# Fixed places for each expert's tokens, with stationary weights, in a state-space scan followed by a top-1 mixture of experts

## The chip, the cores and the metric

The kernel runs on one core of a Trainium2 chip. The core has five engines with queues of their own: TensorE (PE for its matmuls, PEld for its weight loads), VectorE (DVE), ScalarE (ACT), GpSimd (POOL) and SyncE (SP). The metric is the device time of one execution in microseconds (us).

## The reference

The first half is a Mamba-2 scan over 4 sequences of 768 steps with 8 heads, head width 32 and state width 16. The second half routes each of the 3072 tokens to one of 8 experts, which is a two-layer network of width 1024.

```python
# scan, by chunks: y = (C B^T * decay) x  +  (C state) * decay ;  state = decay * state + B^T x
x = attn_out.transpose(0, 2, 1, 3).reshape(3072, 256)      # a token's row
logits = x @ w_gate                                          # 256 -> 8
expert_idx = np.argmax(logits, axis=1)
gate_w = softmax(logits)[np.arange(N), expert_idx]
for e in range(8):
    mask = expert_idx == e
    h = np.maximum(x[mask] @ w1[e], 0.0)                     # 256 -> 1024
    out[mask] = gate_w[mask, None] * (h @ w2[e])             # 1024 -> 256
```

The inputs are drawn with a fixed seed. Everything is fp32 except the counts of the routing.

## The kernel before

**The scan.** The 3072 tokens are 24 chunks of 128. A written-out loop issues, for each chunk: decay factors (`decay`: matmul `abc`, then a VectorE scan into `L`), score products (`scores`: `g` from `ctm` and `bt`), `dec` and `ctd` (`decay_in`), `bs` (`scaled_B`), the mask of the next chunk (`masks`: `ctm`), the state (`state`), the output of the chunk before (`y`), the weighting of `L` (`weigh`), and for the chunk before that the rows by token with their logits (`rows`). GpSimd makes `ctm`, `ctd` and `bs`. Loads come in groups of three chunks on SP's queue, two groups ahead, and the 16 weight matrices (1 MB each) go in the same queue behind them.

**The routing.** For each six chunks `choose` finds the expert and the gate, and SP's queue writes the six chunks' rows to `x_hbm` in token order; two chunks later `rank` numbers the tokens within their experts, with eight VectorE instructions that end in `A_all`.

**The seam.** After the last chunk `table` counts tiles of 128 tokens for each expert and builds, with 24 small matmuls, `idx`: the token in each place of up to 31 tiles, and `ei`, the expert of each tile.

**The experts.** 31 tiles are always run. For each, GpSimd gathers 128 rows by `idx` (`m_gather`, L355), TensorE reads the expert's number into a register (`m_e`, L359) and transposes the rows (`m_xT`, L365), the first product keeps the transposed rows stationary and moves 512 columns of weights (`m_h`, L374), TensorE transposes the result (`m_hT`, L382), the second product keeps the transposed result stationary and moves 256 columns of weights (`m_y`, L389), ACT applies the gate (L392) and GpSimd scatters the rows to the output (L393). TensorE's order is: first product of tile j, transposes of tile j + 1, transposes of h of tile j - 1, second product of tile j - 2. Each fp32 matmul of the code stands in the trace as two instructions, a transpose as one.

Of the kernel before, what the change touches and what calls it, by code (L numbers as in the profile page):

```python
# [9 lines left out]
FP32 = mybir.dt.float32  # L10
# [21 lines left out]
def ssd_then_moe(ctx, tc, x, a, B, BT, CT, w_gate, w1, w2, out):  # L32
    nc = tc.nc
    x_hbm = nc.dram_tensor("x_hbm", (N + 1, W), FP32, kind="Internal").ap()
# [14 lines left out]
    w_all = wpool.tile([128, E, 2, KT * F], FP32, name="w_all")  # L49
# [10 lines left out]
    iota_b = consts.tile([128, 128], BF16, name="iota_b")  # L60
    iota_f = consts.tile([128, 32], FP32, name="iota_f")
    rev_e = consts.tile([128, E], FP32, name="rev_e")
    hi_f = consts.tile([128, NT], FP32, name="hi_f")
    lo_f = consts.tile([128, 1], FP32, name="lo_f")
    zrow = consts.tile([1, W], FP32, name="zrow")

    oh_all = route.tile([128, NT, E], BF16, name="oh_all")
    cnt = route.tile([128, NT + 1, E], BF16, name="cnt")
    rhi_all = route.tile([128, NT], FP32, name="rhi_all")
    A_all = route.tile([128, NT, 128], BF16, name="A_all")  # L70
    idx = route.tile([128, NTILE], I32, name="idx")
    ei = route.tile([1, NTILE], I32, name="ei")

# [13 lines left out]
    def route_consts():  # L87
        nc.gpsimd.memset(Tmat, 1.0)
        nc.gpsimd.affine_select(out=Tmat, in_=Tmat, pattern=[[1, 128]], base=-1, channel_multiplier=-1,
                                compare_op=ALU.is_ge, fill=0.0)  # L90
        nc.gpsimd.memset(ones_bf, 1.0)
        iota_i = sm.tile([128, 128], I32, name="iota_i")
        nc.gpsimd.iota(iota_i, pattern=[[1, 128]], base=0, channel_multiplier=0)
        nc.vector.tensor_copy(iota_b, iota_i)
        nc.vector.tensor_copy(iota_f, iota_i[:, 0:32])
        nc.vector.tensor_scalar(out=rev_e, in0=iota_f[:, 0:E], scalar1=-1.0, scalar2=float(E),
                                op0=ALU.mult, op1=ALU.add)
        nc.vector.tensor_scalar_add(hi_f, iota_f[:, 0:NT], 1.0)
        lo_i = sm.tile([128, 1], I32, name="lo_i")
        nc.gpsimd.iota(lo_i, pattern=[[0, 1]], base=0, channel_multiplier=1)  # L100
        nc.vector.tensor_copy(lo_f, lo_i)
        nc.vector.memset(zrow, 0.0)
        nc.vector.memset(cnt[:, 0, :], 0.0)
        nc.sync.dma_start(out=x_hbm[N:N + 1, :], in_=zrow)

# [29 lines left out]
    def load_w(i):  # L135
        e, u = divmod(i, 2)
        nc.sync.dma_start(out=w_all[:, e, u, :], in_=(w1, w2)[u][e])
# [12 lines left out]
    def decay(k):  # L150
# [3 lines left out]
        for t in range(2):  # L154
# [3 lines left out]
            # L[j, h, i]: the product of a over the steps j + 1 .. i, 1 at i = j, 0 before  # L158
# [73 lines left out]
    rt = [dict() for _ in range(NT // RG)]  # L232

    def rows(k):
# [5 lines left out]
        # columns: features 0 .. 127, logits, features 128 .. 255; the logits add up over both halves  # L240
# [10 lines left out]
    def choose(g):  # L251
# [9 lines left out]
        # of equal logits the first expert  # L261
# [13 lines left out]
        n0 = g * RG * 128  # L275
        nc.sync.dma_start(out=x_hbm[n0:n0 + RG * 128, :].rearrange("(c p) w -> p c w", p=128), in_=r["rows"])

    def rank(g):
# [5 lines left out]
        rk = sm.tile(sh, FP32, name="rk")  # L284
        nc.vector.tensor_tensor(out=rk, in0=p, in1=oh_all[:, sl, :], op=ALU.mult)
# [215 lines left out]
```

## Time and profile before

| | us |
|---|---|
| median of 3 timed runs | 429.83 |
| lowest and highest | 429.77, 429.99 |
| span of the profiled execution | 423.2 |
| TensorE busy (matmuls) | 392.9 |
| VectorE busy | 185.5 |
| GpSimd busy | 115.0 |
| ACT busy | 69.7 |

The span runs from the first to the last instruction of the profiled execution. The page gives no other time for that execution; the timed runs lie 6.6 to 6.8 us above its span. Busy time counts the instructions of an engine, not its waits, and TensorE's matmuls overlap, so that their cost is better read from start to start.

### The profile page before, as it was taken

How to read it: one execution, taken by the hardware profiler on the slowest of the kernel's cores; microseconds unless marked ns; L12 is line 12 of the kernel's file. 1: busy time of each engine (PE TensorE's matmuls, PEld its weight loads, DVE VectorE, ACT ScalarE, POOL GpSimd, SP SyncE). 2: the span in 40 equal slices, each digit the busy share in tenths (PEclk: the TensorE clock that was granted, in tenths of full speed). 3: DMA queues.
4: the chain of work that ended last, by engine and by line, in shares of the span. 5: the costliest groups of instructions: out<-in, count | busy, mean ns of one | idle time of the engine just before them, and what ended most of it. 6: DMA issues, size and time to landing. Idle time of an engine off the chain costs nothing.

```text
span 423.2 us, 5415 instructions
## 1 busy us (share of the span) xinstructions
PE 392.9 (93%) x1879; PEld 247.0 (58%) x1879; DVE 185.5 (44%) x328; ACT 69.7 (16%) x163; POOL 115.0 (27%) x172
## 2 busy tenths in 40 slices
PE   5999999999999813999999999999999999999995
PEld 1355455554554402467767767767767767767773
DVE  5699898889888862113113113113112112112220
ACT  1011110211111210112112112112112112112110
POOL 2333341343333114011231131131131132131011
PEclk9999997998988965899999999999999999999999
DMA  6978859759002021001011010011011011111000
GB/s 192 324 273 323 319 151 363 228 220 254 2 0 76 0 75 51 26 12 39 24 39 35 25 39 28 26 37 30 25 33 39 25 37 37 26 25 29 12 2 0
DMA packets 14498, 37.04 MB, mean 88 GB/s; under 512 B 2278, under 2 KB 9641, under 8 KB 12426
## 3 DMA queue, kind: packets, MB, share of 16 engines
q1 hardware_dynamic: 11498, 29.48, 20.6%
q0 software_dynamic: 2976, 7.23, 6.0%
q8 instruction: 16, 0.26, 0.3%
q14 instruction: 8, 0.07, 0.0%
HBM read 30.40 MB, written 7.22 MB: 89 GB/s over the span
## 4 chain that ended last, share of the span: by engine, by line
issue 53%; PE 17%; POOL 13%; DVE 10%; DMA 4%; POOLq 1%; ACT 0%; SPq 0%; DVEq 0%
POOL xs L355 7%; PE abc L156 6%; PE g L185 4%; DVE L L159 3%; POOL out_dram L393 3%; DVE L L193 3%; DMA w_all<-in_w_dram 2%; PE rows_ps L243 2%; PE y L226 2%; PE A L203 2%; DMA x_hbm<-rows 2%; POOL bs L176 1%; PE y L221 1%; POOL cnt L270 1%; DVE dec L168 1%
## 5 line engine op out<-in xcount | busy, mean ns | idle before, releaser
L374 PE MATMUL h_ps<-w_all,xT 128*128 x248 | 114.0, 603 | 1.0 <-DVE xT L367 1.0
L389 PE MATMUL y_ps<-w_all,hT 128*128 x496 | 112.3, 379 | 0.6 <-ACT yo L392 0.6
L389 PEld LDWEIGHTS y_ps<-w_all,hT 128*128 128x128 f32 x496 | 91.8, 190 | 12.2 <-ACT yo L392 1.0
L367 DVE COPY xT<-xT_ps 128x256 f32<-128x256 f32 x31 | 13.2, 425 | 175.4 <-PE xT_ps L365 169.6
L393 POOL DMA_INDIRECT out_dram<-yo,idx x31 | 31.4, 1012 | 186.7 <-ACT yo L392 186.7
L374 PEld LDWEIGHTS h_ps<-w_all,xT 128*128 128x128 f32 x248 | 47.8, 194 | 49.0 <-issue 45.9
L159 DVE TENSOR_TENSOR_SCAN L<-abc,ident 128x512 f32<-128x512 f32 x48 | 56.0, 1205 | 2.2 <-PE abc L156 2.0
L156 PE MATMUL abc<-az,ident 24*128 24x512 f32 x96 | 51.1, 654 | 4.9 <-DVE az L117 4.9
L377 ACT ACTIVATE h<-h_ps 128x1024 f32<-128x1024 f32 x31 | 31.8, 1025 | 114.1 <-PE h_ps L374 114.1
L384 DVE COPY hT<-hT_ps 128x1024 f32<-128x1024 f32 x31 | 38.0, 1225 | 22.7 <-PE hT_ps L382 22.7
L355 POOL DMA_INDIRECT xs<-x_hbm,idx x31 | 30.3, 977 | 19.2 <-DVE ei L348 10.0
L193 DVE TENSOR_TENSOR L<-g,L 128x512 f32<-128x512 f32 x48 | 30.9, 685 | 10.3 <-POOL bs L176 10.3
L185 PE MATMUL g<-ctm,bt 64*128 64x512 f32 x96 | 32.6, 711 | 2.3 <-POOL ctm L146 2.3
L171 POOL TENSOR_TENSOR ctd<-ct,dec 128x128 f32<-128x128 f32 x24 | 10.9, 455 | 84.2 <-DVE dec L168 70.8
L392 ACT ACTIVATE yo<-y_ps,xs 128x256 f32<-128x256 f32 x31 | 14.7, 473 | 108.0 <-PE y_ps L389 108.0
L382 PE MATMUL hT_ps<-ident,h 128*128 128x128 f32 x248 | 32.1, 273 | 0.0
L156 PEld LDWEIGHTS abc<-az,ident 24*128 24x128 f32 x96 | 17.0, 196 | 22.2 <-issue 15.6
L382 PEld LDWEIGHTS hT_ps<-ident,h 128*128 128x128 f32 x248 | 28.1, 141 | 0.6 <-issue 0.5
L229 ACT COPY yT<-y 128x256 f32<-128x256 f32 x24 | 8.9, 372 | 115.5 <-PE y L226 115.5
L146 POOL TENSOR_TENSOR ctm<-ct,vmask 128x512 f32<-128x512 f32 x24 | 25.0, 1041 | 2.7 <-DVE vmask L84 2.7
L185 PEld LDWEIGHTS g<-ctm,bt 64*128 64x128 f32 x96 | 9.6, 200 | 22.5 <-POOL ctm L146 11.7
L365 PEld LDWEIGHTS xT_ps<-ident,xs 128*128 128x128 f32 x62 | 8.8, 143 | 20.8 <-issue 20.8
(95 smaller groups left out, 223.3 us busy)
## 6 DMA issues: line engine op xcount, KB each, us to landing
w_all<-in_w_dram SPq DMA_DIRECT2D x16, 1024.0 KB, 5.3
x_hbm<-rows SPq DMA_DIRECT2D x4, 771.0 KB
xn<-in_x_dram SPq DMA_DIRECT2D x8, 384.0 KB, 6.7
ct<-in_CT_dram SPq DMA_DIRECT2D x8, 192.0 KB
bt<-in_BT_dram SPq DMA_DIRECT2D x8, 192.0 KB, 2.5
ar<-in_a_dram SPq DMA_DIRECT2D x8, 192.0 KB
bn<-in_B_dram SPq DMA_DIRECT2D x8, 192.0 KB, 6.1
xs<-x_hbm,idx POOLq DMA_INDIRECT x31, 2.8
```

The lines of the kernel that those rows point to most:

```text
L146: nc.gpsimd.tensor_tensor(out=m, in0=bc(at(k, "CT")[:, None, :], [128, 4, 128]), in1=bc(vmask[:, :, None], [128, 4, 128]), op=ALU.mult)
L156: nc.tensor.matmul(p, lhsT=bc(ident[0:NT, k:k + 1], [NT, 128]), rhs=az[:, 4 * t:4 * t + 4, :].rearrange("p h i -> p (h i)"), start=True, s ...
L159: nc.vector.tensor_tensor_scan(out=s["L"][:, 4 * t:4 * t + 4, :].rearrange("p h i -> p (h i)"), data0=p, data1=ident4.rearrange("p h i -> ...
L185: nc.tensor.matmul(g.rearrange("p h i -> p (h i)"), lhsT=at(k, "BT")[sl, :], rhs=s["ctm"][sl].rearrange("p h i -> p (h i)"), start=True, s ...
L193: nc.vector.tensor_tensor(out=d, in0=s["g"][t], in1=d, op=ALU.mult)
L355: nc.gpsimd.indirect_dma_start(out=mt[j]["xs"], out_offset=None, in_=x_hbm[:, :], in_offset=bass.IndirectOffsetOnAxis(ap=idx[:, j:j + 1], ...
L374: nc.tensor.matmul(p[:, f, :], lhsT=mt[j]["xT"][:, t], rhs=w_all[:, ds(mt[j]["e"], 1), 0, c:c + 512], start=(t == 0), stop=(t == KT - 1))
L377: nc.scalar.activation(mt[j]["h"], p.rearrange("p f x -> p (f x)"), func=ACT.Relu)
L382: nc.tensor.transpose(p[:, f], mt[j]["h"][:, 128 * f:128 * f + 128], ident)
L384: nc.vector.tensor_copy(mt[j]["hT"], p)
L389: nc.tensor.matmul(p, lhsT=mt[j]["hT"][:, f], rhs=w_all[:, ds(mt[j]["e"], 1), 1, f * DM:f * DM + DM], start=(f == 0), stop=(f == FT - 1))
L393: s_ = nc.gpsimd.indirect_dma_start(out=out[:, :], out_offset=bass.IndirectOffsetOnAxis(ap=idx[:, j:j + 1], axis=0), in_=yo[:, :], in_offs ...
```

## The change

Each expert gets a region of 3200 rows in `x_hbm`, and its first 448 rows (CAP) are fixed places. `rank` computes a token's position, its rank plus 3200 times its expert, with four VectorE instructions. `place` scatters each chunk's rows to their positions from GpSimd's queue, two chunks at a time behind the masks of three consecutive chunks, and the last six chunks after the loop. A row carries its token's number in a new column (W is 258). The places are first filled with rows that belong to no token, by eight DMAs early in SP's queue. There is no table, no gather and no register for the expert.

In the experts' stage SP loads each expert's three whole tiles of 128 places, and one tile that holds the last 64 places of two experts. The transposed rows of an expert form one tile of 448 columns. The first product keeps the weights stationary and moves the 448 columns, and so gives h transposed. The second product runs for three tiles of an expert, and for two experts' last 64 places together (`m_half`), into the upper and the lower half of one PSUM tile. The order for TensorE is: first product of expert e, transposes of expert e + 2, second product of expert e - 1, after every second expert the halves.

At the end every engine loads a truth value and branches (`over` makes that value from the counts): where an expert has more than 448 tokens, `general` loops over its other tiles.

```diff
-W = DM + 1
-NTILE = N // 128 + E - 1
+W = DM + 2
+CAP = 448
+TT = CAP // 128
+NK = -(-(N - CAP) // 128)
+NR = N + 128
...
-    x_hbm = nc.dram_tensor("x_hbm", (N + 1, W), FP32, kind="Internal").ap()
+    x_hbm = nc.dram_tensor("x_hbm", (E * NR, W), FP32, kind="Internal").ap()
-    w_all = wpool.tile([128, E, 2, KT * F], FP32, name="w_all")
+    w_sb = [[wpool.tile([128, KT * F], FP32, name=f"w{u + 1}_{e}") for u in range(2)] for e in range(E)]
...
+        nc.gpsimd.iota(tok_i, pattern=[[128, NT]], base=0, channel_multiplier=1)
+        nc.gpsimd.memset(zrows, 0.0)
+        none_i = sm.tile([64, CAP // 64], I32, name="none_i")
+        nc.gpsimd.iota(none_i, pattern=[[0, CAP // 64]], base=N, channel_multiplier=0)
+        nc.gpsimd.tensor_copy(zrows[:, :, DM + 1].bitcast(I32), none_i)
+        for e in range(E):
+            nc.sync.dma_start(out=x_hbm[e * NR:e * NR + CAP, :].rearrange("(p c) w -> p c w", c=CAP // 64),
+                              in_=zrows)
...
-        nc.sync.dma_start(out=x_hbm[n0:n0 + RG * 128, :].rearrange("(c p) w -> p c w", p=128), in_=r["rows"])
+        nc.gpsimd.tensor_copy(r["rows"][:, :, DM + 1].bitcast(I32), tok_i[:, g * RG:g * RG + RG])
...
+        nc.vector.tensor_tensor(out=rb, in0=p, in1=bc(base_e[:, None, :], sh), op=ALU.add)
+        nc.vector.tensor_tensor(out=rb, in0=rb, in1=oh_all[:, sl, :], op=ALU.mult)
+        nc.vector.tensor_reduce(rf, rb, axis=AX, op=ALU.add)
+        nc.vector.tensor_copy(pos[:, sl], rf)
+    def place(k):
+        nc.gpsimd.memset(spare, 0.0)
+        s_ = nc.gpsimd.indirect_dma_start(
+            out=x_hbm[:, :], out_offset=bass.IndirectOffsetOnAxis(ap=pos[:, k:k + 1], axis=0),
+            in_=rt[k // RG]["rows"][:, k % RG, :], in_offset=None)
...
+    def over(tb, pp):
...
+    def m_load(e, mo):
+        for t in range(TT):
+            xs = mo.tile([128, W], FP32, name="xs", bufs=4 * TT)
+            r0 = e * NR + 128 * t
+            nc.sync.dma_start(out=xs, in_=x_hbm[r0:r0 + 128, :])
+        if e % 2 == 0:
+            xs = mo.tile([128, W], FP32, name="xh", bufs=3)
+            for u in range(2):
+                r0 = (e + u) * NR + 128 * TT
+                nc.sync.dma_start(out=xs[64 * u:64 * u + 64, :], in_=x_hbm[r0:r0 + 64, :])
+    def xT_of(xs, pp):
+        p = pp.tile([128, KT, 128], FP32, name="xT_ps", tag="xT", bufs=2)
         for t in range(KT):
+            nc.tensor.transpose(p[:, t], xs[:, 128 * t:128 * t + 128], ident)
+        return p
+
+    def m_xT(e, mo, pp):
+        if e % 2 == 0:
+            for u in range(2):
+                ex[e + u]["xT"] = mo.tile([128, KT, CAP], FP32, name="xT", bufs=4)
+            p = xT_of(ex[e]["xh"], pp)
+            for u in range(2):
+                nc.vector.tensor_copy(ex[e + u]["xT"][:, :, 128 * TT:CAP], p[:, :, 64 * u:64 * u + 64])
+        for t in range(TT):
+            p = xT_of(ex[e]["xs"][t], pp)
+            nc.vector.tensor_copy(ex[e]["xT"][:, :, 128 * t:128 * t + 128], p)
...
+    def up(xT, w, f, n, pp):
+        p = pp.tile([128, 512], FP32, name="h_ps", tag="h", bufs=3)
+        for t in range(KT):
+            c = t * F + f * 128
+            nc.tensor.matmul(p[:, 0:n], lhsT=w[:, c:c + 128], rhs=xT[:, t], start=(t == 0), stop=(t == KT - 1))
+    def m_h(e, mo, pp):
+        for f in range(FT):
+            p = up(ex[e]["xT"], w_sb[e][0], f, CAP, pp)
+            nc.scalar.activation(ex[e]["hT"][:, f], p, func=ACT.Relu)
+    def m_half(e, mo, pp):
+        for f in range(FT):
+            for u in range(2):
+                nc.tensor.matmul(p[64 * u:64 * u + 64, :], lhsT=ex[e + u]["hT"][:, f, 128 * TT:CAP],
+                                 rhs=w_sb[e + u][1][:, f * DM:f * DM + DM], start=(f == 0), stop=(f == FT - 1))
...
+            if 0 <= k - 4 - RG < NT - RG and (k - 4) % RG < RG // 2:
+                for i in range(2):
+                    place(k - 4 - RG + (k - 4) % RG + i)
+        for k in range(NT - RG, NT):
+            place(k)
...
+        over(tb, pp)
+        for e in range(2):
+            m_load(e, mo)
+            m_xT(e, mo, pp)
+        for e in range(E + 1):
+            if e < E:
+                m_h(e, mo, pp)
+            if e + 2 < E:
+                m_load(e + 2, mo)
+                m_xT(e + 2, mo, pp)
+            if e > 0:
+                m_y(e - 1, mo, pp)
+            if e % 2 == 1:
+                m_half(e - 1, mo, pp)
+    more = nc.values_load(nk[0:1, E:E + 1], min_val=0, max_val=1, skip_runtime_bounds_check_because="a truth value")
+    with tc.If(more > 0):
+        with tc.tile_pool(name="gp", bufs=1) as gp:
+            general(gp, pp)
```

## Rows read from the trace of the kernel before

**Rows 1.** Busy time by stretch: engines, granted clock, DMA share, GB/s.

```profile
core 0: us, PE busy (x) PEld busy (x) DVE busy (x) ACT busy (x) POOL busy (x), PEclk, DMA share, GB/s
0.00:149.88 149.88, 139.99 (x798) 70.84 (x799) 125.01 (x227) 23.02 (x100) 52.09 (x104) 0.94 0.57 192
149.88:167.13 17.25, 2.60 (x29) 1.83 (x28) 9.82 (x40) 0.25 (x2) 4.57 (x10) 0.54 0.20 61
167.13:418.59 251.46, 250.33 (x1052) 174.32 (x1052) 50.70 (x61) 45.95 (x61) 57.33 (x58) 0.99 0.10 28
418.59:423.16 4.57, 0.00 (x1) 0.00 (x0) 0.00 (x0) 0.47 (x1) 0.98 (x1) 0.77 0.01 0
```

**Rows 2.** The page's chain of waits, shares of the span by engine.

```profile
issue 53%; PE 17%; POOL 13%; DVE 10%; DMA 4%; POOLq 1%; ACT 0%; SPq 0%; DVEq 0%
```

**Rows 3.** Timeline of one tile: start us, us, engine, line, operation, count, idle before.

```profile
386.04 3.60 PE L374 MATMUL h_ps<-w_all,xT 128*128 x8
...
389.48 0.38 PE L365 MATMUL xT_ps<-ident,xs 128*128 128x128 f32 x2
...
389.69 1.04 PE L382 MATMUL hT_ps<-ident,h 128*128 128x128 f32 x8
...
389.89 0.42 DVE L367 COPY xT<-xT_ps 128x256 f32<-128x256 f32 x1 [5.88 <-PE xT_ps L365]
...
390.57 3.62 PE L389 MATMUL y_ps<-w_all,hT 128*128 x16
...
394.02 3.60 PE L374 MATMUL h_ps<-w_all,xT 128*128 x8
```

**Rows 4.** Timeline of TensorE in the scan, the y product of one chunk.

```profile
22.46 0.64 PE L226 MATMUL y<-L,xn 128*32 128x128 f32 x16
```

**Rows 5.** Timeline of the seam: rank, a gather, and the first product.

```profile
152.85 0.21 DVE L285 TENSOR_TENSOR rk<-rank,oh_all 128x48 f32<-128x48 f32 x1 [1.22 <-PE rank L283]
...
165.59 0.95 POOL L355 DMA_INDIRECT xs<-x_hbm,idx  x1 [0.30 <-issue]
...
167.13 6.04 PE L374 MATMUL h_ps<-w_all,xT 128*128 x8 [0.52 <-DVE xT L367]
```

**Rows 6.** Timeline of VectorE, first and last of a rank's eight instructions.

```profile
69.41 0.21 DVE L285 TENSOR_TENSOR rk<-rank,oh_all 128x48 f32<-128x48 f32 x1 [0.52 <-PE rank L283]
...
70.50 0.96 DVE L295 TENSOR_TENSOR A_all<-iota_b,rlo 128x768 bf16<-128x768 bf16 x1
```

**Rows 7.** Timeline of GpSimd in two chunks of the scan.

```profile
84.45 0.46 POOL L171 TENSOR_TENSOR ctd<-ct,dec 128x128 f32<-128x128 f32 x1 [3.03 <-DVE dec L168]
84.86 0.41 POOL L176 TENSOR_TENSOR bs<-bn,L 128x128 f32<-128x128 f32 x1
...
89.72 0.59 POOL L176 TENSOR_TENSOR bs<-bn,L 128x128 f32<-128x128 f32 x1
```

**Rows 8.** Busy time by stretch, while the first groups are loaded.

```profile
10.00:15.00 5.00, 5.00 (x8) 1.66 (x8) 3.60 (x6) 0.00 (x0) 1.82 (x3) 1.00 0.96 270
```

**Rows 9.** Timeline of GpSimd, the masks of chunks 0 and 6.

```profile
5.60 1.15 POOL L146 TENSOR_TENSOR ctm<-ct,vmask 128x512 f32<-128x512 f32 x1 [2.73 <-DVE vmask L84]
...
39.17 1.03 POOL L146 TENSOR_TENSOR ctm<-ct,vmask 128x512 f32<-128x512 f32 x1
```

**Rows 10.** DMA queues (packets, MB, share) and issues (count, KB, us to landing).

```profile
q8 instruction: 16, 0.26, 0.3%
...
bt<-in_BT_dram SPq DMA_DIRECT2D x8, 192.0 KB, 2.5
...
out_dram<-yo,idx POOLq DMA_INDIRECT x31, 2.1
```

**Rows 11.** Timeline of SP's queue, one load issued.

```profile
7.02 0.43 SPq L133 DMA_DIRECT2D xn<-in_x_dram  x1
```

**Rows 12.** Instructions of the tile `ei`: duration in ns, least, median and longest.

```profile
L359 PEldq TENSOR_LOAD <-ei x31: 295/301/496, 162.9 to 390.4; - x31
```

**Rows 13.** Timeline of TensorE in the scan, behind a wait.

```profile
62.61 2.46 PE L185 MATMUL g<-ctm,bt 64*128 64x512 f32 x4 [0.88 <-POOL ctm L146]
```

**Rows 14.** Busy time by stretch, around that wait.

```profile
60.00:80.00 20.00, 19.12 (x103) 10.22 (x103) 17.24 (x31) 2.83 (x15) 6.25 (x10) 0.83 0.84 271
```

More of the change, by code (lines that the diff above doesn't have):

```diff
@@ L136, in load_w @@
         e, u = divmod(i, 2)
-        nc.sync.dma_start(out=w_all[:, e, u, :], in_=(w1, w2)[u][e])
+        nc.sync.dma_start(out=w_sb[e][u], in_=(w1, w2)[u][e])
     def at(k, nm):
@@ new lines, in rank @@
+        nc.vector.tensor_copy(pos[:, sl], rf)
[4 more added lines that the diff above has]
+            in_=rt[k // RG]["rows"][:, k % RG, :], in_offset=None)
+        tc.declare_no_dep(s_.ins, group="pl", reason="each token has a place of its own: the rows are disjoint")
+        tc.add_to_no_dep_group("pl", s_.ins)
+    def over(tb, pp):
+        cn = pp.tile([128, E], FP32, name="cn", tag="y", bufs=2)
+        nc.tensor.matmul(cn, lhsT=ones_bf, rhs=cnt[:, NT, :], start=True, stop=True)
+        ov = tb.tile([128, E], FP32, name="ov")
+        nc.vector.tensor_scalar(out=ov, in0=cn, scalar1=float(127 - CAP), scalar2=0.0, op0=ALU.add, op1=ALU.max)
+        nc.vector.tensor_copy(nk[:, 0:E], ov)
+        nc.vector.tensor_scalar(out=nk[:, 0:E], in0=nk[:, 0:E], scalar1=7, scalar2=None, op0=ALU.logical_shift_right)
+        fl = tb.tile([128, 2], FP32, name="fl")
+        nc.vector.tensor_reduce(fl[:, 0:1], ov, axis=AX, op=ALU.max)
+        nc.vector.tensor_scalar(out=nk[:, E:E + 1], in0=fl[:, 0:1], scalar1=127.0, scalar2=None, op0=ALU.is_gt)
+        nc.vector.tensor_copy(nk[:, E + 1:], cn)
@@ new lines, in put @@
+    def put(p, xs, mo):
+        yo = mo.tile([128, DM], FP32, name="yo", bufs=3)
+        nc.scalar.mul(yo, p, xs[:, DM:DM + 1])
+        s_ = nc.gpsimd.indirect_dma_start(
+            out=out[:, :], out_offset=bass.IndirectOffsetOnAxis(ap=xs[:, DM + 1:DM + 2].bitcast(I32), axis=0),
+            in_=yo[:, :], in_offset=None, bounds_check=N - 1, oob_is_err=False)
+        tc.declare_no_dep(s_.ins, group="sc", reason="each token stands in one place: the rows are disjoint")
+        tc.add_to_no_dep_group("sc", s_.ins)
@@ new lines, in general @@
+    def general(gp, pp):
+        for e in range(E):
+            r = nc.values_load(nk[0:1, E + 1 + e:E + 2 + e], engines=[ENG.SP], min_val=0, max_val=N,
+                               skip_runtime_bounds_check_because="a count of at most N tokens")
+            for u in range(2):
+                nc.sync.dma_start(out=x_hbm[ds(r + (e * NR + 64 * u), 64), :], in_=zrows[:, 0, :])
+        for e in range(E):
+            n_e = nc.values_load(nk[0:1, e:e + 1], min_val=0, max_val=NK,
+                                 skip_runtime_bounds_check_because="tiles of at most N - CAP places")
+            with tc.For_i(0, n_e) as k:
+                xs = gp.tile([128, W], FP32, name="g_xs")
+                nc.sync.dma_start(out=xs, in_=x_hbm[ds(k * 128 + (e * NR + CAP), 128), :])
+                p = xT_of(xs, pp)
+                xT = gp.tile([128, KT, 128], FP32, name="g_xT")
+                nc.vector.tensor_copy(xT, p)
+                hT = gp.tile([128, FT, 128], FP32, name="g_hT")
+                for f in range(FT):
+                    nc.scalar.activation(hT[:, f], up(xT, w_sb[e][0], f, 128, pp), func=ACT.Relu)
+                p = pp.tile([128, DM], FP32, name="y_ps", tag="y", bufs=2)
+                for f in range(FT):
+                    nc.tensor.matmul(p, lhsT=hT[:, f], rhs=w_sb[e][1][:, f * DM:f * DM + DM],
+                                     start=(f == 0), stop=(f == FT - 1))
+                yo = gp.tile([128, DM], FP32, name="g_yo")
+                nc.scalar.mul(yo, p, xs[:, DM:DM + 1])
+                nc.gpsimd.indirect_dma_start(
+                    out=out[:, :], out_offset=bass.IndirectOffsetOnAxis(ap=xs[:, DM + 1:DM + 2].bitcast(I32), axis=0),
+                    in_=yo[:, :], in_offset=None, bounds_check=N - 1, oob_is_err=False)
```

161 lines of the change are left out of this document (25 added, 136 removed).

## The prediction, made before the changed kernel was run

> **What bounds the kernel now.** I first cut the span into four stages with the table of busy time by stretch [rows 1]. The reader is to see where TensorE's busy time fills the stretch. The scan ends at 149.88 us; then comes a seam of 17.25 us in which TensorE works 2.60 us, while VectorE builds the table of tiles and GpSimd starts the gathers; the experts take 251.46 us, of which TensorE is busy 250.33; the end is 4.57 us. The chain of waits calls 53% "issue" and 13% GpSimd [rows 2], which in the experts' stage follows the gathers and scatters; that is misleading, since TensorE hardly waits there. So in that stage only TensorE's own work counts; in the seam every step counts; in the scan VectorE (125.01 of 149.88 us busy) and TensorE share the path.
>
> The timeline of one tile prices TensorE's work from start to start, which leaves the overlapped ends out [rows 3]: first product 3.44 us for 8 instructions of 512 columns (430 ns each, 0.84 ns a column; the code has 4, so an fp32 matmul is two instructions), two transposes of x 0.21, eight transposes of h 0.88, second product 3.45 for 16 instructions of 256 columns (216 ns). A tile is 7.98 us and 31 of them 247.4; the other 4 us of the stage are a cold start and two small waits.
>
> **The experts, part by part.** *Removed:* the transposes of h, 31 x 0.88 = 27.3 us, because the first product now makes h already transposed. *Changed:* 31 tiles of 128 rows (3968) become 8 x 448 = 3584 places. First product: 8 experts x 8 blocks x 2 x 2 instructions = 256, each 448 x 0.84 = 376 ns: 96.3 us, against 106.6. Its weight loads change place with the data, but each still has a longer matmul to hide under, as now. Second product: 24 whole tiles x 3.45 = 82.8. The 64-row halves of two experts go, in 32 instructions of 256 columns, to the upper and lower 64 output rows of one tile: 32 x 216 ns = 6.9 us a pair if they run one after the other, 3.45 if side by side. The nearest row is the scan's y product: 16 instructions of 128 columns that write 32 output rows each take 0.64 us together [rows 4], where 16 full ones would take 1.76 (0.110 each, as the transposes of h). Narrow outputs that differ in place do overlap, so I take 4 x 3.45 = 13.8, and keep 27.6 as the other end.
>
> *Transposes of x:* 42 inside the stage (experts 2 to 7; a pair has 14) at 0.105: 4.4. They come in a burst with two PSUM buffers, and VectorE's copy of one takes 0.42 [rows 3]; so the third of a burst waits for the first copy: about 0.45 us for an odd expert, 0.75 for an even one (four bursts), 3.6 in all; nothing if the copies keep up, up to 8.8 if each of the 21 were waited for in full. ACT's ReLU was 1.02 us for 1024 columns and now has 1.5 us for 448, three buffers deep: nothing. *Cold start:* the first eight matmuls take 6.04 us instead of 3.44 [rows 5]; I keep 2.5. Sum: 96.3 + 82.8 + 13.8 + 4.4 + 3.6 + 2.5 = 203.4, **48.1 less**.
>
> **The scan.** *Rank:* eight VectorE instructions, from 69.41 to 71.46, 2.05 us [rows 6], become four of about 0.23: 1.1 less, in three of the four ranks 3.4 (the fourth is in the seam). VectorE's next scan and the weighting queue behind them. *Places:* the write of rows leaves SP's queue and becomes 24 scatters in GpSimd's, 18 of them inside the scan, two per chunk in nine chunks, each with a small memset. Behind them queue ctd, bs and the next ctm, and bs is what VectorE's weighting waits for. The gathers of now follow one another every 1.25 us (0.95 and an idle 0.30 [rows 5]); with the memset 1.35, so two are 2.7 us. GpSimd's idle time before ctd is 3.03 us in an ordinary chunk [rows 7]. It fits, with 0.3 us to spare; if a scatter slowed as bs does (0.41 to 0.59 us), two would take 3.5 or more and each of nine chunks come 0.5 late, 4.5 us. I take 0.9 for this, so the scan gives **2.5 less** (ends: 3.4 less, 1.1 more, or 2.1 with the memset below).
>
> The Trainium skill (GPSIMD Engine Reference, section 8, Key points) says that GpSimd shares its SBUF interfaces with VectorE and contends with instructions of two SBUF inputs. The two durations of bs agree; no row shows a scatter under that load. By the rule the scan would be 1.1 us longer, not 2.5 shorter.
>
> *Zero fill:* eight DMAs, 8 x 448 x 258 x 4 bytes = 3.70 MB, on SP's queue ahead of the third group of loads. At 270 GB/s [rows 8] they take 13.7 us. A group of loads is 1.18 MB (four of 192 KB as bt's [rows 10], one of twice that); with two groups ahead and a start near 2 us the third lands near 2 + 7.24 MB / 270 GB/s = 29 us; its first user is the mask of chunk 6 at 39.17 [rows 9]. Hidden with 10 us to spare; later loads have more, since SP loses the wait for the rows. On GpSimd the memset for it, 1806 elements, stands ahead of the first ctm, before which GpSimd sits idle for 2.73 us [rows 9]; at ctm's own rate (1.03 us for 512) it would be 3.7. I take nothing; 1.0 is the other end.
>
> **The seam.** *Removed:* the table, the 24 small matmuls and the first gather. *Added:* the last six places, which must land before any load of x. Positions are ready four VectorE steps after 152.85: 153.8 [rows 5]. Six scatters at 1.35: the sixth starts at 160.7 and lands 2.1 later (as the output's do [rows 10]), 162.8. SP then issues eight loads at 0.43 each [rows 11], the last at 165.8, landed 2.5 later [rows 10] at 168.3. The order puts all fourteen transposes of experts 0 and 1 ahead of the first product; the last three bursts, paced by copies, take 2: first product at 170.4, against 167.13. **3.3 more** (0.5 if loads and transposes overlap better, 6 if each step is slow).
>
> **The end.** *Added:* every engine loads one register and branches over the general loop. The reference's own inputs give the experts 343 to 418 tokens, so no loop runs. No row shows a branch. Below it is the register load, 0.3 us [rows 12]. Above: the register load at its longest 0.5, a block of instructions (16 pieces in 0.3% of 16 engines' span, 1.3 us each) with a landing of 2.5 [rows 10], and a second ending, at most 2.5 (4.57 less the output's landing): 6.8. Eight loops with their barriers are long code, so I take **4 more**.
>
> The Trainium skill (Runtime: NRT & Kernel Launch, section Instruction fetch mechanics) says that prefetch is sequential and a taken branch to a target outside the window stalls for a fetch. It speaks against this change: with it the sum is as above, without it 3 us less.
>
> **Sum.** 423.16 - 2.5 + 3.3 - 48.1 + 4 = 379.9 us of span. The page gives the profiled execution's span alone; the runs' median lies 6.7 above it, which I keep: 386.5 us.
>
> **Rivals.** *Halves one after the other:* 13.8 more, 400. For: the overlap seen is of 32-row outputs, and no row shows 64. Against: those four ran together without loss. 0.12. *Scatters crowd GpSimd in the scan:* the waits that they make for TensorE bring the clock down, as after the 0.88 us wait at 62.61 [rows 13], when the clock of 60 to 80 us was 0.83 [rows 14]: 6.8 us at half, 3.4 lost. With 3.6 more for the scatters and two further falls, 397. 0.12. *A dear end:* an entry barrier besides, 10 us instead of 4, 392. 0.10. *Clock falls in the experts:* the bursts of transposes leave gaps of 0.45 to 0.75 us; a fall like that one costs 3.4 us, six of them 20: 407. Against: the stage's clock is 0.99 now with its waits for x's transposes in it [rows 1]. 0.05. *Slower than before:* the same mechanism, but the clock stays at its lower level of 1.2 GHz after each burst. The products are 193 us of work at full clock and a microsecond of it at half clock costs another; the gain of 43.3 is gone when each of six bursts is followed by 14.4 us at half clock, twice that fall of the scan. All of it at half clock would be 580 us. 0.03.
>
> **How the numbers follow.** My own sum has 0.56, with a range of 379 to 394: down by the waits for copies (3.6) and the cheap end (3.7), up by all that the copies could add (5.2) and a slow seam (2.7). The rest (0.02) is below 378, all lower ends at once being 373. The range of 378 to 401 leaves out the clock's two rivals and the rest, 0.10, and the upper edge of the halves. Every case but the last ends below 429.83; about 0.2% is what a measurement of this kernel can tell from no change: faster 0.96, same 0.01, slower 0.03.
>
> **What will show it.** The page of the changed kernel should have the first product at 376 ns an instruction from start to start and no wait of its own; the halves' 32 instructions in about 3.5 us; GpSimd's idle time before ctd near 0.3 us in nine chunks; six scatters 1.35 apart in the seam and the first product near 168; and 8 to 9 us from the last matmul to the end. I am wrong if the products' clock falls, if weight loads show between matmuls, or if the stretch behind the last output grows past 10 us.

## The result, and the profile after

The changed kernel takes 385.87 us (median of 4 runs, 385.45 to 388.67), the kernel before 429.91 (median of 4 runs, 429.77 to 430.22). The ratio is 0.9016, with a 95% interval of 0.8959 to 0.9073: faster. The forecast was 386.5 us, with a range of 378 to 401. The profiled execution took 386.13 us at a span of 384.4.

The table of busy time by stretch, cut at the same events as [rows 1] (last copy of logits, first product, last matmul, end). Columns: stretch and its length, busy time of the engines, granted clock, DMA share, GB/s.

```profile
0.00:148.87 148.87, 137.66 (x798) 68.74 (x799) 121.36 (x211) 22.93 (x100) 70.79 (x142) 0.95 0.64 215
148.87:173.72 24.85, 4.33 (x17) 2.68 (x17) 5.64 (x25) 0.25 (x2) 10.39 (x24) 0.55 0.40 120
173.72:377.16 203.44, 201.31 (x811) 134.68 (x810) 8.70 (x25) 47.53 (x91) 26.57 (x27) 1.00 0.08 26
377.16:384.42 7.26, 0.00 (x0) 0.00 (x0) 0.00 (x0) 0.47 (x1) 0.98 (x1) 0.69 0.08 25
```

The gain is all but 1.01 us in the third row, 203.44 us instead of 251.46, where TensorE is still busy nearly all the time (201.31 us) at the higher of its two clock levels (2.4 GHz, 1.00 granted). The seam grew by 7.60 us, the end by 2.69, and the scan fell by 1.01. In sum that is 38.7 us of span, while the medians differ by 44.0: the profiled execution of the kernel before was a short one (423.2 us; the fast runs of that kernel beside the experiments have spans from 421.5 to 428.0), and no trace of a longer one was kept. The chain of waits now reads "issue 52%; PE 19%; POOL 17%", much as [rows 2] did, and tells as little about where the time went.

The experts, in the timeline: transposes of x for a pair, first product of expert 1, transposes for an odd expert, second product, halves. This answers to [rows 3].

```profile
186.47 0.38 PE L333 MATMUL xT_ps<-ident,xh 128*128 128x128 f32 x2
186.69 0.38 PE L333 MATMUL xT_ps<-ident,xs 128*128 128x128 f32 x2
187.48 0.72 PE L333 MATMUL xT_ps<-ident,xs 128*128 128x128 f32 x4 [0.41 <-PE xT_ps L333]
188.04 12.19 PE L351 MATMUL h_ps<-xT,w 128*128 128x448 f32 x32
200.07 0.60 PE L333 MATMUL xT_ps<-ident,xs 128*128 128x128 f32 x4
200.97 0.44 PE L333 MATMUL xT_ps<-ident,xs 128*128 128x128 f32 x2 [0.30 <-DVE xT L345]
201.25 10.53 PE L373 MATMUL y_ps<-w,hT 128*128 128x256 f32 x48
211.70 3.67 PE L382 MATMUL y_ps<-w,hT 128*64 128x256 f32 x32
215.31 1.02 PE L351 MATMUL h_ps<-xT,w 128*128 128x448 f32 x2
```

From start to start the first product takes 12.03 us for 32 instructions, 376 ns each, and the halves 3.61 for 32 instructions of 256 columns, hardly more than 16 full ones cost in a row (10.45 / 3 = 3.48). The bursts of transposes take 1.57 us for a pair (four tiles) and 1.18 for an odd expert (three); without a wait, at 0.21 us a tile, they would take 0.85 and 0.64.

The seam, on GpSimd, SP and TensorE (it answers to [rows 5]):

```profile
144.73 1.03 POOL L294 DMA_INDIRECT x_hbm<-rows,pos  x1 [0.16 <-POOL spare L293]
...
151.13 0.96 POOL L294 DMA_INDIRECT x_hbm<-rows,pos  x1 [0.22 <-issue]
152.12 1.59 POOL L272 TENSOR_TENSOR cnt<-cnt,oh_all 128x8 bf16<-128x8 bf16 x6
...
155.42 1.00 POOL L294 DMA_INDIRECT x_hbm<-rows,pos  x1 [1.56 <-DVE fl L309]
156.73 0.97 POOL L294 DMA_INDIRECT x_hbm<-rows,pos  x1 [0.22 <-issue]
...
161.82 0.97 POOL L294 DMA_INDIRECT x_hbm<-rows,pos  x1 [0.22 <-issue]
```
```profile
164.85 1.28 SPq L321 DMA_DIRECT2D xs<-x_hbm  x3
166.17 1.15 SPq L327 DMA_DIRECT2D xh<-x_hbm  x2
```
```profile
169.50 0.66 PE L333 MATMUL xT_ps<-ident,xh 128*128 128x128 f32 x2 [15.27 <-DMA xs<-x_hbm]
169.96 0.64 PE L333 MATMUL xT_ps<-ident,xs 128*128 128x128 f32 x2
170.85 3.08 PE L333 MATMUL xT_ps<-ident,xs 128*128 128x128 f32 x10 [0.26 <-PE xT_ps L333]
173.72 12.91 PE L351 MATMUL h_ps<-xT,w 128*128 128x448 f32 x32
```

The reader is to see that the six scatters of the third group of chunks (144.73 to 151.13) stand ahead of the last counts, that SP's first load starts 3.03 us after the last scatter's start, and that the fourteen transposes take 4.22 us.

### The profile page after: what moved, and what is told of

Same layout as the page of the kernel before. It is cut to its first block, busy times and chain, and to the rows that moved or that the text cites. A ratio compares the mean times of both kernels' runs of the same rounds, so it can differ in the third digit from the quotient of the medians.

```text
span 384.4 us, 4487 instructions
## 1 busy us (share of the span) xinstructions
PE 343.3 (89%) x1625; PEld 206.1 (54%) x1625; DVE 135.7 (35%) x261; ACT 71.2 (19%) x193; POOL 108.7 (28%) x193
## 4 chain that ended last, share of the span: by engine, by line
issue 52%; PE 19%; POOL 17%; DVE 8%; DMA 1%; POOLq 1%; SPq 0%; DVEq 0%
POOL out_dram L363 7%; PE abc L158 6%; PE g L187 5%; POOL x_hbm L294 4%; DVE L L161 3%; DVE L L195 3%; PE A L205 2%; PE y L228 2%; POOL bs L178 2%; PE rows_ps L245 2%; POOL ctm L148 1%; POOL cnt L272 1%; PE y L223 1%; POOL ctd L173 1%; DMA x_hbm<-rows,pos 1%
## 5 line engine op out<-in xcount | busy, mean ns | idle before, releaser
L351 PE MATMUL h_ps<-xT,w 128*128 128x448 f32 x256 | 98.6, 544 | 0.0
L373 PE MATMUL y_ps<-w,hT 128*128 128x256 f32 x384 | 84.3, 380 | 0.0
L373 PEld LDWEIGHTS y_ps<-w,hT 128*128 128x128 f32 x384 | 72.7, 190 | 10.5 <-issue 1.1
L363 POOL DMA_INDIRECT out_dram<-yo,xs x24 | 23.6, 984 | 178.1 <-ACT yo L362 178.1
L351 PEld LDWEIGHTS h_ps<-xT,w 128*128 128x128 f32 x256 | 48.8, 192 | 46.2 <-issue 46.1
L358 ACT ACTIVATE hT<-h_ps 128x448 f32<-128x448 f32 x64 | 34.8, 543 | 89.3 <-PE h_ps L351 89.3
L294 POOL DMA_INDIRECT x_hbm<-rows,pos x24 | 23.7, 987 | 6.2 <-issue 4.2
L245 PE MATMUL rows_ps<-turn,yT 128*128 128x136 f32 x96 | 18.1, 313 | 0.6 <-ACT lg L250 0.6
L228 PE MATMUL y<-L,xn 128*32 128x128 f32 x384 | 16.3, 288 | 0.4 <-DVE L L195 0.4
L205 PEld LDWEIGHTS A<-xn,bs 128*128 128x128 f32 x40 | 6.8, 212 | 18.1 <-issue 9.1
```

The costliest lines, as they stand in the source:

```text
L228: nc.tensor.matmul(p[D * q:D * q + D, t], lhsT=at(k, "x")[:, D * h:D * h + D], rhs=s["L"][:, h], start=(not inter and t == 0), stop=True, ...
L245: nc.tensor.matmul(p[:, 128 * t:128 * t + 128 + E], lhsT=st[k]["yT"][:, t], rhs=turn[:, (128 + E) * t:(128 + E) * (t + 1)], start=(t == 0) ...
L294: s_ = nc.gpsimd.indirect_dma_start(out=x_hbm[:, :], out_offset=bass.IndirectOffsetOnAxis(ap=pos[:, k:k + 1], axis=0), in_=rt[k // RG]["ro ...
L351: nc.tensor.matmul(p[:, 0:n], lhsT=w[:, c:c + 128], rhs=xT[:, t], start=(t == 0), stop=(t == KT - 1))
L358: nc.scalar.activation(ex[e]["hT"][:, f], p, func=ACT.Relu)
L363: s_ = nc.gpsimd.indirect_dma_start(out=out[:, :], out_offset=bass.IndirectOffsetOnAxis(ap=xs[:, DM + 1:DM + 2].bitcast(I32), axis=0), in_ ...
```

## The experiments

Stage lengths of the experiments are read as above, the experts' stage up to the start of the last gate on ACT (203.5 us in the changed kernel, 251.5 before), the end from there (7.2 and 4.5). A ratio is that to the kernel before, run beside it; for four runs (short branch, halves apart, tokens stationary, scatters behind the scan) this comparison is on record as unclear, and what is read from them rests on their stages. The scan has two lengths in these kernels, which differ by when TensorE's rate doubles near the start (last section): 148.9 us in the profile of the changed kernel and 151.5 where it doubles late. Scans are compared with scans of the same kind; that of the kernel before (149.9) is of the early kind.

**No branch.**
```diff
-    with tc.If(more > 0):
-        with tc.tile_pool(name="gp", bufs=1) as gp:
-            general(gp, pp)
```


> Leaves out the register load, the branch and the general loop behind it (with these inputs no expert needs it). Theory: the branch costs about what the trace of the changed kernel shows behind the landing of the last output, a register load of 0.38 us and a compare-and-branch of 0.88 us with the second ending, so the stretch from the last matmul to the end falls from 7.26 us to 4.6 us, as before, and the time by about 2.5 us to 383.4; nothing else moves. Rival one: the branch is free beside the ending of the program, and the time stays within 0.5 us. Rival two: the code of eight loops costs more elsewhere, as instructions that are loaded, and the time falls by 5 us or more.

The end took 4.4 us instead of 7.2, so the branch costs 2.8. The median did not show it: 386.32 us (ratio 0.903, interval 0.8972 to 0.9088). The profiled execution, 386.1 us, had the long scan, 151.5 us; the other five have no trace, but the two shortest spans, 381.4 and 381.5 us, lie 2.1 us or more below the lowest of the changed kernel, 383.6. The first theory holds for the end; the median was no fit measure for it.

**A short branch.**
```diff
-        for e in range(E):
+        for e in range(1):
```
(in both loops of `general`)

> The branch stays, but the general loop behind it serves one expert instead of eight, so its code is an eighth as long (with these inputs it does not run). Theory: what the branch costs is the register load and the jump, not the length of what is jumped over, so the stretch from the last gate to the end stays at 7.2 us within 0.3. Rival: the jump over long code waits for instructions to be fetched, and over short code it does not; then the stretch falls to about 5.5 us or less (4.4 without a branch).

The end took 5.3 us (5.34 against 7.17; the eight other traces with the long branch have 6.85 to 7.27), so the rival holds: 1.8 us of the branch's 2.8 go with the length of the code that is jumped over. ACT's branch and its next instructions, first of the changed kernel, then with the short branch; columns: durations in ns (least, median, longest), first and last start in us:

```profile
L479 ACTq COMPARE_BRANCH  x1: 50/50/50, 377.8 to 377.8; - x1
L479 ACTq EVENT_SEMAPHORE  x2: 17/17/17, 380.8 to 380.9; - x2
```
```profile
L479 ACTq COMPARE_BRANCH  x1: 50/50/50, 381.7 to 381.7; - x1
L479 ACTq EVENT_SEMAPHORE  x2: 17/17/17, 382.2 to 382.3; - x2
```

From the branch to the next instruction it takes 3.0 us with the long code and 0.45 with the short (on GpSimd 2.9 and 0.5). Not all of these 2.5 us reach the end: with the short code the ending waits for the last scatter to land instead, until 384.9 us. DMA queues of instructions in the last stretch, first of the changed kernel (377 to 384.4 us), then with the short branch (380 to 386.4 us); columns: packets, MB, share of 16 engines:

```profile
q14 instruction: 4, 0.03, 1.7%
q8 instruction: 1, 0.02, 0.8%
```
```profile
q14 instruction: 2, 0.02, 0.6%
```

Five packets of instructions against two; without a branch there is none in the last stretch. The Trainium skill (Runtime: NRT & Kernel Launch, section Instruction fetch mechanics) says that a taken branch to a target outside the current window of instructions stalls for a fetch. The trace agrees: 3.0 us against 0.45, and three packets more.

**Halves apart.**
```diff
-        for f in range(FT):
-            for u in range(2):
+        for u in range(2):
+            for f in range(FT):
```


> Only the order of the 16 matmuls for the shared tile changes: all of the upper 64 rows, then all of the lower 64. Theory: the halves ran side by side because consecutive matmuls wrote different output rows, so apart each pair takes 6.9 us instead of 3.5, four pairs 13.8 us more: 399.7 us, all of it in the experts' stage (203.4 to about 217). Rival: each matmul is cheap for having 64 columns of stationary data, wherever its neighbour writes; then the stage stays at 203 and the time at 386.

```profile
214.55 6.31 PE L382 MATMUL y_ps<-w,hT 128*64 128x256 f32 x32
220.79 12.29 PE L351 MATMUL h_ps<-xT,w 128*128 128x448 f32 x32
```

A pair took 6.24 us instead of 3.61, the experts' stage 213.9 us instead of 203.5, the time 398.72 (ratio 0.9315). The order alone decides. In the changed kernel two neighbours start 6 ns apart and the next two 216 ns later, so neighbours that write different halves of the output rows run side by side. Apart, the matmuls of one half start 216 ns behind one another, as full ones do; only the first four of the lower half ran beside the last four of the upper, which makes 195 ns in the mean and the loss 10.3 us instead of the 13.8 of the theory. The Trainium skill (TensorEngine Tiling (Array Packing), section Tiling Modes, Key Properties) says that different tiles of the array can execute in parallel; the trace agrees, with a factor of 1.73 (6.24 to 3.61 us).

**Tokens stationary.** The first product, second product and transposes of h as in the kernel before, on 28 tiles of the fixed places (`TL` lists them, the shared tile of a pair last); the branch and the general loop are left out:
```diff
...
+                for u in range(2 if t == TT else 1):
+                    nc.tensor.matmul(p[sl, f, :], lhsT=mt[j]["xT"][:, q, sl], rhs=w_sb[e + u][0][:, c:c + 512],
+                                     start=(q == 0), stop=(q == KT - 1))
...
+            nc.tensor.transpose(p[:, f], mt[j]["h"][:, 128 * f:128 * f + 128], ident)
```


> Keeps the fixed places, the shared tiles and the loads, but the first product goes back to stationary tokens and moving weights, tile by tile in the old order, with eight transposes of h for each tile; the general loop is left out. 28 tiles instead of the old 31. Theory: a tile costs the old 7.98 us, so the stage takes 28 x 7.98 + 4 = 227 us, 24 more than with stationary weights and 24 less than before; with a seam that is shorter by about 4 us (one tile is transposed ahead of the first product, not seven) and an end that is 2.5 shorter, 404 us. Half of the gain of the change in the experts' stage is then the tile count, half the transposes. Rival one: the transposes hide beside the matmuls, the gain came from the tile count alone, and the stage takes 206 us, the time about 383. Rival two: the tile count gave nothing (the stage was bound by gathers and scatters), the stage stays near 250 us, the time near 427.

```profile
300.12 3.60 PE L351 MATMUL h_ps<-w,xT 128*128 128x512 f32 x8
303.55 0.38 PE L338 MATMUL xT_ps<-ident,xs 128*128 128x128 f32 x2
303.77 1.04 PE L359 MATMUL hT_ps<-ident,h 128*128 128x128 f32 x8
304.64 3.62 PE L369 MATMUL y_ps<-w,hT 128*128 128x256 f32 x16
308.10 3.60 PE L351 MATMUL h_ps<-w,xT 128*128 128x512 f32 x8
```

A tile is 7.98 us, as in [rows 3] (8.07 to 8.22 around a shared tile); the stage took 230.0 us, 3 more than forecast, the seam 18.9, the time 403.92 (ratio 0.9477). Both rivals fail. So of the 48.0 us that the stage gained, 21.5 came with the smaller number of tiles, what sharing costs included, and 26.5 with the stationary weights. Most of the latter is the transposes of h that they save, by the row of one tile 28 x 0.88 = 24.6 us.

**Three buffers for the rows.**
```diff
-            r["rows"] = wk.tile([128, RG, W], FP32, name="rows")
+            r["rows"] = wk.tile([128, RG, W], FP32, name="rows", bufs=3)
```


> Three buffers instead of two for the rows of six chunks. Theory: the copy of chunk 14's rows at 93.39 us waited 3.92 us for a buffer whose scatters had not landed, and this made the scan 2.1 us late; with a third buffer no copy waits for a scatter, the idle time of ACT there goes, and the scan falls from 148.9 to about 146.8 us, the time to 383.8. Rival: the wait only shows where VectorE and the clock would have lost the time anyway; the scan stays within 0.5 us of 148.9.

In the changed kernel's timeline of ACT and GpSimd the wait and its result stand so:

```profile
93.39 0.27 ACT L248 COPY rows<-rows_ps 128x128 f32<-128x128 f32 x1 [3.92 <-DMA x_hbm<-rows,pos]
```
```profile
97.70 0.45 POOL L173 TENSOR_TENSOR ctd<-ct,dec 128x128 f32<-128x128 f32 x1 [3.87 <-DVE dec L170]
```

With three buffers the copy at this place waits 0.20 us, and from `bs` of chunk 14 to that of chunk 15 it takes 7.0 us instead of 9.1 (6.9 before the change). The scan took 149.3 us; this execution had the late start, with which the run without a branch needed 151.5. So 2.2 us came back, as the theory had it. By its letter the rival's sign came true as well (149.3 is within 0.5 us of 148.9), but only because the start was another; the wait ahead of `ctd` of chunk 15, 3.87 us above and 1.75 with three buffers, does not hang on the start. The median of 385.12 does not resolve it.

**Scatters behind the scan.** Three row buffers, and
```diff
-        for k in range(NT - RG, NT):
+        for k in range(RG, NT):
             place(k)
```
with only the first group's pairs left in the loop.

> Three buffers for the rows, and the scatters of the second and third group go behind the loop, so that 6 instead of 18 stand in the scan. Theory: a pair of scatters fits into GpSimd's idle time of 3.0 us per chunk and costs a chunk at most 0.3 us, so the scan falls by no more than 1 us against three buffers alone (chunks 17 to 23), and the seam grows by the twelve scatters, 15.3 us, less what the tail held already (about 7): time about 395. Rival: the scatters crowd GpSimd in the scan, a chunk with a pair comes 0.5 us or more later, and from chunk 17 on the scan is 3 us or more shorter without them.

Scan 148.8 us against 149.3 with three buffers alone (both with the late start), seam 37.0, time 397.09 (ratio 0.9303). Twelve scatters fewer in the loop are worth 0.5 us: the first theory. But only six of the twelve had stood between chunks; the six of the third group start behind the last `bs` (143.84 us with three buffers alone, the scatters from 144.62). So what a pair costs a chunk is tested by three chunks, not by nine. The seam grew by 12.7 us and not by the 8 of the theory, because all eighteen scatters now stand behind the last counts.

**Scatters a chunk earlier.**
```diff
-            if 0 <= k - 4 - RG < NT - RG and (k - 4) % RG < RG // 2:
+            if 0 <= k - 3 - RG < NT - RG and (k - 3) % RG < RG // 2:
```
(and the same index in `place`)

> Each pair of scatters inside the loop goes one chunk earlier, right behind the rank that gives its positions, so the six of the third group are issued before the last chunk's work ends. Theory: the last counts (cnt) started 3.25 us after the last logits instead of 1.35 because six scatters stood ahead of them in GpSimd's queue; issued earlier they no longer do, the seam falls from 24.85 to about 22.9 us. Rival: GpSimd then waits for the positions in the loop and delays ctd and bs, and what the seam gains the scan loses (a chunk with scatters comes 0.5 us or more later, nine of them).

```profile
144.18 0.17 DVE L290 CAST pos<-rf 128x6 int32<-128x6 f32 x1
```
```profile
145.16 1.03 POOL L294 DMA_INDIRECT x_hbm<-rows,pos  x1 [3.68 <-DVE pos L290]
...
152.35 0.96 POOL L294 DMA_INDIRECT x_hbm<-rows,pos  x1 [0.21 <-issue]
154.64 1.57 POOL L272 TENSOR_TENSOR cnt<-cnt,oh_all 128x8 bf16<-128x8 bf16 x6 [1.34 <-DVE oh_all L269]
```

Both came true. The counts now start 1.3 us after the last logits and the seam took 22.7 us, 2.1 less; but the scatter behind the rank blocks GpSimd's queue (3.68 us idle), and the scan took 153.4 us, 1.9 more than with the same start (0.4 of it stood already at chunk 3). The blocked queue cost more than that, for this run is also rid of the wait for a row buffer: no copy of rows waits longer than 0.25 us near 93 us, and from `bs` of chunk 14 to that of chunk 15 it takes 7.0 us. The time is 387.91 (ratio 0.9057). The rows also explain another wait: the scatter starts 0.81 us after the end of `pos` (144.35). In the changed kernel `pos` ends at 154.61 and the first place starts 0.81 later, at 155.42; the page's releaser `fl` there is a neighbour in time, and the 0.81 us belongs to a scatter that has waited for its index.

**Order in the seam.**
```diff
         for e in range(2):
             m_load(e, mo)
-            m_xT(e, mo, pp)
+        m_xT(0, mo, pp)
         for e in range(E + 1):
             if e < E:
                 m_h(e, mo, pp)
+            if e == 0:
+                m_xT(1, mo, pp)
```
(with the load of `xh` ahead of those of `xs`)

> The tile of the last 64 places is loaded first, and the transposes for expert 1 go behind expert 0's first product. Theory: the first product waited for seven tiles, three of them not needed by it, transposed at half clock, 0.72 us a tile, and for the shared tile that was loaded fourth and transposed first; the seam falls from 24.85 to about 21 us, and the experts' stage grows by about 1.2 us, a burst at full clock: 2.7 us less in sum. Rival: the clock rises only after TensorE has worked for a while; then the first product runs longer at half clock by what the transposes no longer cover, and the sum of both stages stays within 1 us of 228.3.

```profile
170.49 0.66 PE L333 MATMUL xT_ps<-ident,xh 128*128 128x128 f32 x2 [13.63 <-DMA xh<-x_hbm]
171.15 2.02 PE L333 MATMUL xT_ps<-ident,xs 128*128 128x128 f32 x6
173.69 13.90 PE L351 MATMUL h_ps<-xT,w 128*128 128x448 f32 x32 [0.52 <-DVE xT L345]
187.42 0.60 PE L333 MATMUL xT_ps<-ident,xs 128*128 128x128 f32 x4
```

Seam 22.2 us, experts 206.0: 228.2 in sum against 228.4. The rival holds in its sum, and in part in its reason. The first 32 instructions took 13.73 us here, 12.75 in the changed kernel and 12.03 at full clock; the granted clock is 0.50 until 176.95 us here and until 175.17 in the changed kernel, 3.3 and 1.5 us into the product. So 1.0 of what the seam won was paid by the product, and 1.5 by the burst behind it, which with seven tiles takes 3.08 us instead of 1.57. The time is 388.64 (ratio 0.9076), no gain.

**Three PSUM buffers for the transposes.**
```diff
-        p = pp.tile([128, KT, 128], FP32, name="xT_ps", tag="xT", bufs=2)
+        p = pp.tile([128, KT, 128], FP32, name="xT_ps", tag="xT", bufs=3)
```


> Three PSUM buffers for the transposes of x instead of two. Theory: in the experts' stage an odd expert's burst takes 1.18 us where its matmuls need 0.64, an even one's 1.57 where they need 0.85, because the third tile waits for the first copy; with a third buffer the odd ones lose the wait, the even ones most of it, and the stage falls from 203.5 to about 200.5 us, the seam by about 0.5. Rival: VectorE's copies pace the burst anyway and the next product waits for the last of them; then the stage stays within 0.5 us of 203.5.

```profile
185.68 0.38 PE L333 MATMUL xT_ps<-ident,xh 128*128 128x128 f32 x2
...
186.69 0.41 PE L333 MATMUL xT_ps<-ident,xs 128*128 128x128 f32 x2 [0.19 <-PE xT_ps L333]
186.94 12.19 PE L351 MATMUL h_ps<-xT,w 128*128 128x448 f32 x32
198.97 0.82 PE L333 MATMUL xT_ps<-ident,xs 128*128 128x128 f32 x6
199.62 0.60 PE L373 MATMUL y_ps<-w,hT 128*128 128x256 f32 x2
```

Bursts of 1.26 and 0.65 us instead of 1.57 and 1.18; the experts' stage fell to 201.3 us and the seam to 23.8, 3.3 in all; 383.85 us (ratio 0.8989, interval 0.893 to 0.9048). The waits for copies were real: an odd expert's are gone, of an even one's 0.72 us 0.41 are left.

**Fill twice.**
```diff
-        for e in range(E):
-            nc.sync.dma_start(out=x_hbm[e * NR:e * NR + CAP, :].rearrange("(p c) w -> p c w", c=CAP // 64),
+        for e in range(2 * E):
+            r0 = (e % E) * NR
+            nc.sync.dma_start(out=x_hbm[r0:r0 + CAP, :].rearrange("(p c) w -> p c w", c=CAP // 64),
                               in_=zrows)
```


> Writes the fill of the places twice, 7.4 MB instead of 3.7 ahead of the third group of loads. Theory: the fill is hidden because the third group is needed only at 39 us and was issued at 23 us; a second fill blocks SP for another 15 us, to about 38.5 us, so that chunk 6 and those behind it come about 4 us later (2 to 7), and the slack that this eats was the 10 us which the forecast named. Rival one: the loads have more room still, and no chunk is later by over 0.5 us. Rival two: the fill also slows the weights and the scatters for longer, and the scan loses 10 us or more.

The eight DMAs of the fill block SP from 8.08 to 23.28 us in the changed kernel; the sixteen here:

```profile
8.07 33.09 SPq L106 DMA_DIRECT2D x_hbm<-zrows  x16
41.20 2.19 SPq L128 DMA_DIRECT2D ct<-in_CT_dram  x1
```
```profile
47.65 1.04 POOL L149 TENSOR_TENSOR ctm<-ct,vmask 128x512 f32<-128x512 f32 x1 [4.46 <-DMA ct<-in_CT_dram]
```

The mask of chunk 6 waited 4.46 us for its load, and `bs` of chunk 7 came 5.1 us later than in the run without a branch, which had the same start. The scan took 157.3 us, 5.8 more, the time is 394.39 (ratio 0.9244). A single fill has its slack: in the changed kernel the first load of the third group is issued at 23.32 us and lands at 30.6, 8.6 us ahead of the mask of chunk 6 at 39.22. The forecast had 29 and 10 us to spare.

**Four small edits together:** three buffers for the rows, three for the transposes, and
```diff
...
+                    if q < NT - RG - 2:
+                        place(q)
+            if k == NT + 1:
+                for q in range(NT - RG - 2, NT - RG):
+                    place(q)
...
+            if e == 0:
+                over(tb, pp)
```
(`over` no longer ahead of the loads)

> Four small edits together, each with its own place in the trace: three buffers for the rows, three PSUM buffers for the transposes of x, the last two scatters of the third group behind the last counts, and the count for the branch taken behind expert 0's first product. Theory: the chunk that waited for a buffer loses 2 us, the experts' stage falls to about 201.3 us and the seam by 1.0 (both as seen with three PSUM buffers alone); in the seam the counts start 1.4 us after the last logits instead of 3.25, which is worth 1.1 us because GpSimd's twelve scatters then stand without a gap, and the first place no longer waits 0.8 us for the count. Seam about 21.9 us, time 379 to 381.5 (there are two lengths of the scan, 2.6 us apart, by when TensorE's rate doubles near the start). Rival: the scatters behind the counts push the last six back by their own time (2.5 us), and the seam stays at 23.8 us.

Scan 145.7 us (with the early start), seam 23.0, experts 201.0, end 7.2: 379.93 us (377.74 to 382.21; ratio 0.8915, interval 0.8862 to 0.8969). Its six spans, 376.0 to 380.5, lie below the changed kernel's four, 383.6 to 386.9, so it is shorter than both kernels, than the changed one by 1.5% of the median. The time lies in its range, but the parts do not all: the scan gained 3.1 us where 2 were expected, and the seam missed its 21.9. The counts did start 1.3 us after the last logits, and the first of the last six scatters no longer waited; but two more scatters now stand behind the counts, eight filled GpSimd's queue without a gap, and the last started 12.3 us after the scan's end instead of 13.0. The push that the rival named took back most of what the counts gained.

## Why the prediction was right

The time was right, and so was the mechanism of its largest term. That the sum came within 0.6 us is luck: two errors elsewhere, of 4.5 and 5.0 us, cancelled.

**The experts: 203.4 forecast, 203.44 measured.** 376 ns for an instruction came as worked out, and three second products (10.45 us) and a pair of halves (3.61) within 5% of it. The waits for copies were forecast at 3.6; the excess of the bursts, 0.72 and 0.54 us for three each, is 3.8, and with a third buffer the stage lost 2.2. The cold start was put at 2.5; the first product lost 0.7 (12.75 against 12.03), for the transposes ahead of it had taken most of the time at half clock, in the seam. That the total agrees to 0.04 us is luck too: first products 96.5 (forecast 96.3), second products 83.5 (82.8), halves 14.4 (13.8) and bursts 8.2 (8.0) make up for the 1.8 of the cold start. That the halves ran side by side was shown by setting them apart: 10.3 us more, so this rival's 13.8 was somewhat high. The bursts brought no fall of the clock (1.00 granted over the stage).

**The scan: 2.5 less forecast, 1.0 measured.** The removed half of the rank gave 2.5 us over three ranks, by the starts of `bs` of chunks 11, 17 and 23; the forecast had 3.4. Another 1.0 came at chunk 20, where the clock of the kernel before was granted at 0.50 from 117.3 to 120.7 us and that of the changed kernel at 1.00; whether the change brought that is not shown. Scatters fitted into GpSimd's idle time: 0.5 to 1.0 us were left ahead of `ctd` in the six chunks behind a pair, more than the 0.3 forecast for nine (the last three pairs came behind the last `ctd`); they cost 0.3 us by the starts of `bs`, not 0.9, and the 24 scatters took 0.96 to 1.18 us, with a median of 0.97, so VectorE's work hardly slowed them. What the step missed is a wait through a buffer: the rows' tile has two buffers and is now read by scatters instead of one early write, and at 93.39 us ACT waited for a scatter to land, 2.1 us for the scan. The third buffer took it back. Without this wait the scan would have been 3.1 us shorter.

**The seam: 3.3 more forecast, 7.6 measured; this is the step that failed.** Its parts against the forecast: counts behind six scatters of the third group, 1.9 late (their cover was the last chunks' idle time, which is not there behind chunk 23); 0.8 for the first scatter after its wait; scatters 1.28 apart, not 1.35, 0.5 less (0.15 of it a slip in the forecast's sum, 153.8 + 5 x 1.35 is 160.55); 3.0 instead of 2.1 from the last scatter to SP's first load, 0.9; and loads and transposes 8.9 instead of 7.6, 1.3, with the clock at its lower level of 1.2 GHz (0.50 granted from the first transpose to the first product). They sum to 4.4. The first was shown by issuing the scatters earlier. Of the last, three PSUM buffers took 1.2 back (7.7 us from SP's first load to the first product), so it was waits for copies; the order of the seam gained nothing in sum. The 0.8 and the 0.9 are read from rows and not tested by a run of their own.

**The end: 4 forecast, 2.7 measured.** The branch costs 2.8, and 1.8 of it goes with the length of the code, as the prediction supposed when it took more than the register load.

**The fill** was hidden, and doubling it showed that this rested on slack. One figure was wrong without consequence: by the reference's inputs the experts have 336 to 418 tokens, not 343 to 418. None has more than 448, so no run shows what `general` costs when it is needed.

**The sum.** Scan 1.5, seam 4.3 and end -1.3 make the span 384.4 instead of 379.9, 4.5 more. The 6.7 us between span and time were 1.7. The step was wrong in kind: it compared the span of one execution with the median of others. In the runs of the kernel before that went with the experiments each time lies 2.1 to 2.2 above its own span (425.37 beside 423.2, 429.69 beside 427.5), and it is the spans that differ. The two errors left 0.4 us to the profiled execution's 386.13, 0.6 to the median.

## What to carry to other kernels

Price TensorE's work from start to start and count instructions; where TensorE filled its stage here, such a sum held to one per cent for the full products. In a seam, list each queue's contents at the moment when the last item arrives: work that was free behind a chunk is in the way when no chunk follows. When a write is moved to a later place, ask how long it keeps its source buffer, and compare a span only with the time of the same execution.

## What the runs showed of the hardware

**The rate of TensorE at the start.** The same four matmuls of chunk 2, first in the changed kernel, then without a branch:

```profile
18.46 1.98 PE L158 MATMUL abc<-az,ident 24*128 24x512 f32 x4
```
```profile
18.68 3.78 PE L158 MATMUL abc<-az,ident 24*128 24x512 f32 x4
```

TensorE's first matmul starts at 5.13 us in the changed kernel and at 5.11 in the other, and its instructions took twice their later time until about 18 us in the one and about 27 in the other. The table by stretch shows a granted clock of 1.00 there, but the trace holds no record of the clock for that time, and a stretch without one is shown as 1.00: the first record, of the full level, starts at 18.16 us in the changed kernel and at 26.92 without a branch, which is when the instructions become faster. In five of the thirteen traces here this first record starts between 17.6 and 19.1 us, in eight between 26.0 and 27.6. `bs` of chunk 3 comes at 28.44 and 32.56 us, the scan's end 2.6 us apart. What decides it stays open; no run here was made to settle it. It is as large as the effects of 2 us that the medians did not show, so that the stages of the trace had to be read instead.

**The jump over unused code** costs by the length of that code: 5.3 us of end for one expert's loops, 7.2 for eight, 4.4 for none. Lengths between were not run.
